# One joined instruction in the float64 conversion, x loaded in 1 KB rows, and a new order of the first loads

## The chip, the cores and the metric

The kernel runs on one core of one Trainium2 chip. The metric is the device time of one execution in microseconds (us). The engines are PE (TensorE matmul; PEld is its weight load), DVE (VectorE), ACT (ScalarE), POOL (GpSimd) and SP (SyncE, which here only issues DMAs).

## The reference, cut to what matters

Attention over 8 batches, 8 heads, 512 rows, 32 state rows and 64 features is followed by two gated products. The weights come as float64 arrays, x and state as float32.

```python
scores = scale * x @ state.T            # [B, H, 512, 32]
xread = softmax(scores, -1) @ state     # each row of x reads the state
sread = softmax(scale * state @ x.T, -1) @ x   # each state row reads x
x = concat([xread, sread], axis=2)      # per batch 544 rows of 512
h = (x @ w1) * (x @ w2) @ w3            # 512 -> 1024 -> 1024
x2 = h @ w_out                          # 1024 -> 512
out = (x2 @ w_a) * (x2 @ w_b) @ w_out2  # 512 -> 1536 -> 512
```

## The kernel before, in words

All tiles of 128 x 1024 four-byte words come from a pool of 47 units; PSUM is a pool of 8 banks. Every large product runs as three passes over a high and a low part (`PASSES`), so that each operand is split by an ACT cast (`high`, L305, or L147) and a subtraction on DVE or POOL (`low`, L311, or L153).

**Start.** The weights w1 and w2 are multiplied by the state before anything else (`state_product`, L326, tile pb), and these products go to DRAM (`p_d`) and come back as chunks pr (`load_p`, L602). w3 and w_out are multiplied into one matrix (`transpose_w3`, L355; `weight_product`, L370, tile wp). Attention of batches 0 and 1 is made beside it, then the first batch's two gated products (`first_product`, tile f, recorded at L1129) and its output (`first_output`, L1366, tile x2f). All of this is a list of `Job` objects, each with an engine, an assumed duration, what it waits for, how many free units and banks it needs and a priority; `run_jobs` puts them in an order by these assumed times, and each engine then executes its instructions in that order. `EARLY` gives the order of the loads on SP: `w3_i` and `woi` are 1 MB pieces of w3 and w_out, `wkp_nh` are halves of the rows of w1 and w2 for two heads, `xb` is batch b. `WO_ORDER`, the order in which a weight product takes its w_out pieces, follows from `EARLY`. `KEEP`, `KEEP_SG`, `LATE_KEEP` and the like say how many units stay free.

**Conversion of float64 (class `Convert`).** A piece of 128 x 512 values has a high word c and a low word d per value. `take` runs two ACT instructions in place (L178 on c, L181 on d), `shift` a DVE instruction (L187, c shifted left by 3 into a new tile) and `add` a POOL instruction (L193, d added). There are 40 such pieces in the start and 52 later, in the intakes sw (w1, w2 once more), ab (w_a, w_b) and z (w_out2), which call `make`.

**Attention.** `load_x_half` brings four heads in four DMAs, with 256-byte runs; `x_transpose` transposes 128 x 128 blocks (two heads of 64 features on the partitions); `scores` multiplies the state's transposed tile `st_s` with it, per head, 64 x 32 weights over 512 columns; `scores_move` copies each of two banks to SBUF on ACT; `maxima`, `col_exp`, `row_shift` and so on are the softmax in both directions. `MIDDLE` and `BEHIND` place these steps of batch b+1 and b+2 between the products of batch b from batch 1 on.

**Later.** `block1` (tiles ap, bp, hfp, hp, x2p) runs batches 1 to 7 and the state rows, 24 passes per step; the intakes and `Features` work beside it. `block2(g)`, four times, holds the second gated product (L1583), its state part for g = 0 (`state_step`, L1666) and the output (L1909). Only g = 0 still has conversions beside it.

Of the kernel before, what the change touches and what calls it, by code (L numbers as in the profile page):

```python
# [9 lines left out]
F32 = mybir.dt.float32  # L10
# [14 lines left out]
    "w3_6 wo0 w3_0 w3_7 wo2 w3_2 w3_4 x0 wo3 w3_3 wo1 "  # L25
    "w3_5 x1 w3_1 wk1_0 wk0_0 wk1_1 x2 wk3_0 wk2_1 wk2_0 wk0_1 wk3_1"
# [38 lines left out]
P_KEEP = 3  # L65
X_SLOT = 0
PASSES = ((0, 0), (0, 1), (1, 0))
# [3 lines left out]
def attention_moe_moe2(  # L71
# [93 lines left out]
    class Convert:  # L165
# [9 lines left out]

        def take(self, i):
            c, d = self.words(i)
            nc.scalar.activation(  # L178
                out=c.bitcast(F32), in_=c.bitcast(F32), func=AF.Prelu, scale=2.0**-112, alpha=2.0**32
            )  # L180
            nc.scalar.activation(out=d.bitcast(I32), in_=d, func=AF.Copy, scale=2.0**-29)  # L181

        def shift(self, i):
            if self.out is None:
                self.out = unit(self.name)[:, : self.n]
            c, out = self.words(i)[0], self.out[:, i * 512 : (i + 1) * 512].bitcast(U32)
            nc.vector.tensor_scalar(  # L187
                out=out, in0=c, scalar1=3, scalar2=None, op0=ALU.logical_shift_left
            )

        def add(self, i):
            d, out = self.words(i)[1], self.out[:, i * 512 : (i + 1) * 512].bitcast(I32)
            nc.gpsimd.tensor_tensor(out=out, in0=out, in1=d.bitcast(I32), op=ALU.add)  # L193
            free(self.raws[i][0])

        def make(self):
            for i in range(len(self.raws)):
                self.shift(i)
                self.add(i)
# [23 lines left out]
    def load_x_half(b, g):  # L223
        t = unit(f"x{b}_{g}")
        v = t.rearrange("p (t h d) -> p t h d", h=4, t=NT)
# [19 lines left out]
    st_s = unit("stT")  # L245

# [31 lines left out]
    def state_move(bg):  # L278
        nc.scalar.copy(st_s[:, bg * 512 : (bg + 1) * 512], st_b[bg])
# [109 lines left out]
    class Attention:  # L389
# [5 lines left out]
        def x_transpose(self, g):  # L395
            self.xt.append(flat(unit(f"xt{self.b}_{g}"), S))
            for j in range(2):
                t = self.banks[g, j] = bank(f"xt{self.b}_{g}_{j}")
                for n in range(NT):
                    nc.tensor.transpose(  # L400
# [1576 lines left out]
```

## Time and profile before

| | us |
|---|---|
| median of 3 runs (1310.37 to 1311.49) | 1310.57 |
| the profiled execution | 1310.82 |
| its span, first to last instruction | 1309.0 |
| PE busy in the span | 1275.8 |
| DVE, ACT, POOL busy | 748.8, 584.4, 582.2 |

PE is busy for 97% of the span, and its granted clock is 0.994 on average. The span therefore has 33 us in which PE does nothing, and the question for each stage is how much of these lie in it and who ends them.

### The profile page before, as it was taken

How to read it: one execution, taken by the hardware profiler on the slowest of the kernel's cores; microseconds unless marked ns; L12 is line 12 of the kernel's file. 1: busy time of each engine (PE TensorE's matmuls, PEld its weight loads, DVE VectorE, ACT ScalarE, POOL GpSimd, SP SyncE). 2: the span in 40 equal slices, each digit the busy share in tenths (PEclk: the TensorE clock that was granted, in tenths of full speed). 3: DMA queues.
4: the chain of work that ended last, by engine and by line, in shares of the span. 5: the costliest groups of instructions: out<-in, count | busy, mean ns of one | idle time of the engine just before them, and what ended most of it. 6: DMA issues, size and time to landing. Idle time of an engine off the chain costs nothing.

```text
span 1309.0 us, 19764 instructions
## 1 busy us (share of the span) xinstructions
PE 1275.8 (97%) x7514; PEld 1079.3 (82%) x7514; DVE 748.8 (57%) x861; ACT 584.4 (45%) x956; POOL 582.2 (44%) x398
## 2 busy tenths in 40 slices
PE   6998999999999999999999999999999999999998
PEld 4765777878877888988879998889988889988898
DVE  5896044767566667555656853247922369433493
ACT  7896355555555666455433431123511235212232
POOL 5674125545355487367348341148411274212450
PEclk7999999999999999999999999999999999999999
DMA  9988695564676642698574779317695247873271
GB/s 305 291 246 260 186 269 181 178 176 137 193 221 206 216 142 86 250 304 275 193 289 145 250 257 386 113 36 248 222 405 175 65 166 260 339 270 107 81 257 66
DMA packets 155134, 276.56 MB, mean 211 GB/s; under 512 B 47136, under 2 KB 92192, under 8 KB 155040
## 3 DMA queue, kind: packets, MB, share of 16 engines
q1 hardware_dynamic: 150752, 260.09, 60.1%
q0 software_dynamic: 4288, 15.21, 3.0%
q8 instruction: 60, 0.98, 0.3%
q14 instruction: 34, 0.28, 0.1%
HBM read 205.00 MB, written 70.25 MB: 210 GB/s over the span
## 4 chain that ended last, share of the span: by engine, by line
PE 81%; DVE 3%; ACT 2%; DMA 2%; issue 1%; POOL 1%; SPq 0%; ACTq 0%
PE r L1583 19%; PE ro L1909 10%; PE x2p L1188 10%; PE v L1583 9%; PE vo L1909 5%; PE bp L1129 5%; PE ap L1129 5%; PE q L1583 5%; PE qo L1909 2%; PE abs L1666 2%; PE x2f L1366 2%; PE srv L1848 1%; PE pb L326 1%; PE bs L1129 1%; DMA zr<-in_moe_w_out_dram 1%
## 5 line engine op out<-in xcount | busy, mean ns | idle before, releaser
L1772 POOL TENSOR_TENSOR r<-e,e 128x512 f32<-128x512 f32 x48 | 63.6, 1325 | 278.5 <-DVE e L1597 278.5
L1188 PE MATMUL x2p<-hp,ws 128*128 128x512 f32 x672 | 161.9, 390 | 0.0
L1188 PEld LDWEIGHTS x2p<-hp,ws 128*128 128x128 f32 x672 | 125.7, 188 | 26.3
L153 POOL TENSOR_TENSOR pl<-pr,ph 128x512 fp32r<-128x512 f32 x64 | 84.5, 1341 | 137.1 <-ACT ph L147 106.2
L1717 ACT COPY e<-r 128x512 f32<-128x512 f32 x48 | 28.2, 588 | 188.7 <-PE r L1583 188.6
L1780 DVE TENSOR_TENSOR r<-e,r 128x512 f32<-128x512 f32 x48 | 33.0, 687 | 128.8 <-PE r L1583 128.8
L1153 DVE TENSOR_TENSOR hfp<-asbp,bp 128x512 f32<-128x512 f32 x56 | 38.2, 683 | 82.7 <-PE bp L1129 81.6
L153 DVE TENSOR_TENSOR hp<-hfp,hp 128x512 fp32r<-128x512 f32 x56 | 55.2, 986 | 41.9 <-ACT hp L147 41.2
L1597 DVE TENSOR_TENSOR e<-e,q 128x512 f32<-128x512 f32 x48 | 32.9, 685 | 73.3 <-PE q L1583 73.3
L1621 POOL TENSOR_TENSOR r<-r,r 128x1024 f32<-128x1024 f32 x24 | 70.9, 2967 | 2.2 <-issue 1.2
L1583 PE MATMUL r<-xT3h,w 128*128 128x512 f32 x192 | 67.1, 390 | 2.0 <-ACT e L1745 2.0
L1583 PE MATMUL r<-xT4h,w 128*128 128x512 f32 x192 | 67.3, 391 | 1.2 <-DVE e L1597 1.2
L1583 PE MATMUL r<-xB11h,w 128*128 128x512 f32 x192 | 67.0, 390 | 0.2 <-DMA w<-w_d 0.2
L1583 PE MATMUL r<-xT2h,w 128*128 128x512 f32 x192 | 67.2, 390 | 0.0
L1583 PE MATMUL q<-xB21h,w 128*128 128x512 f32 x192 | 66.9, 389 | 0.0
L1583 PE MATMUL v<-xB22h,w 128*128 128x512 f32 x192 | 66.9, 389 | 0.0
L1583 PE MATMUL v<-xT1h,w 128*128 128x512 f32 x192 | 66.9, 389 | 0.0
L147 ACT CAST hp<-hfp 128x512 fp32r<-128x512 f32 x56 | 34.7, 619 | 62.5 <-DVE hfp L1153 61.1
L1745 ACT COPY e<-r 128x512 f32<-128x512 f32 x48 | 28.2, 588 | 70.8 <-PE r L1583 70.8
L1147 ACT COPY asbp<-ap 128x512 f32<-128x512 f32 x56 | 33.0, 589 | 49.7 <-PE ap L1129 49.7
L1597 DVE TENSOR_TENSOR e<-e,v 128x512 f32<-128x512 f32 x48 | 32.9, 685 | 29.2 <-PE v L1583 22.8
L1129 PE MATMUL bp<-ah,ph 128*128 128x512 f32 x112 | 47.9, 428 | 0.3 <-DVE a L485 0.3
(503 smaller groups left out, 3821.5 us busy)
## 6 DMA issues: line engine op xcount, KB each, us to landing
w<-w_d SPq DMA_DIRECT2D x132, 512.0 KB, 7.9
zz<-z_d SPq DMA_DIRECT2D x84, 512.0 KB, 4.4
w_d<-w SPq DMA_DIRECT2D x96, 256.0 KB, 3.4
p_d<-sg SPq DMA_DIRECT2D x128, 128.0 KB, 2.6
pr<-p_d SPq DMA_DIRECT2D x32, 512.0 KB, 5.5
w<-w_d SPq DMA_DIRECT2D x36, 256.0 KB, 9.0
x<-in_x_dram SPq DMA_DIRECT2D x64, 128.0 KB, 4.5
sw<-in_moe_w_dram SPq DMA_DIRECT2D x16, 512.0 KB, 5.1
```

The lines of the kernel that those rows point to most:

```text
L147: nc.scalar.copy(hi, src)
L153: (eng or nc.vector).tensor_tensor(out=lo[:, i], in0=src[:, i], in1=hi[:, i].bitcast(F32), op=ALU.subtract)
L1129: nc.tensor.matmul(dst[:, :n], lhsT=l[m], rhs=r[q], start=i == 0 and j == 0, stop=i == k - 1 and j == 2,)
L1147: nc.scalar.copy(a_sb[:, :n], pa[:, :n])
L1153: nc.vector.tensor_tensor(out=hf[:, :n], in0=a_sb[:, :n], in1=pb[:, :n], op=ALU.mult)
L1188: nc.tensor.matmul(acc[j], lhsT=w_s[f][:, m, j * P : (j + 1) * P], rhs=h[:, q, :n], start=per == 1 and f == 0 and i == 0, stop=f == NF1 - ...
L1583: nc.tensor.matmul(t, lhsT=w[m], rhs=xf[g].parts[x][q][:, k, :], start=first and k == 0 and i == 0, stop=k == 1 and i == 2, skip_group_che ...
L1597: nc.vector.tensor_tensor(out=out, in0=x, in1=y, op=ALU.add)
L1621: ENGINES[eng].tensor_tensor(out=out, in0=x, in1=y, op=op)
L1772: nc.gpsimd.tensor_tensor(out=h[1], in0=e2, in1=e5, op=ALU.mult)
L1780: nc.vector.tensor_tensor(out=h[0], in0=e1, in1=r, op=ALU.mult)
L1909: nc.tensor.matmul(dst, lhsT=hl[m][:, k, i * P : (i + 1) * P], rhs=z[:, k, q, :], start=FIRST[p] and j == 0 and k == 0 and i % 2 == 0 and ...
```

## The change

1. The conversion's last two steps become one DVE instruction (`join`: shift c left by 3, then OR with d), for all 92 pieces; POOL's add goes. So that an OR does, d's scale is reduced (`LAST_BITS`).
2. In the start, d's step (`last_bits`) may run on ACT or POOL, the casts `high` and the copies of x (`x_part`) on ACT or DVE, whichever the plan finds earlier. In the intakes `take` stays on ACT.
3. x comes with one DMA for four heads, in runs of 1 KB. After the transposes the partitions then hold two neighbouring rows of one head. Each head's scores are made from both halves of the partitions, so there is a second state tile with the halves exchanged (`stX`, two DVE copies from PSUM for each of two groups), `scores` issues 16 products of 256 columns in place of 8 of 512, and `scores_move` writes in pieces of 128 columns.
4. The order of the loads, the priorities and the units kept free are new. The state is loaded behind the first w3 piece, not between its halves. The third load is a w_out piece, x of batch 0 the fourth, an attention weight the sixth; the last two are `wk0_0` and `w3_0`.
5. A transposed half of w3 waits for its own half's conversion only. The intake z looks 2.0 us ahead in place of 1.5.

```diff
 EARLY = (
-    "w3_6 wo0 w3_0 w3_7 wo2 w3_2 w3_4 x0 wo3 w3_3 wo1 "
-    "w3_5 x1 w3_1 wk1_0 wk0_0 wk1_1 x2 wk3_0 wk2_1 wk2_0 wk0_1 wk3_1"
+    "w3_6 w3_3 wo3 x0 w3_4 wk0_1 wo0 x2 w3_7 x1 wo1 "
+    "wo2 wk1_1 wk2_0 w3_2 w3_5 wk1_0 wk3_1 wk3_0 wk2_1 w3_1 wk0_0 w3_0"
 ).split()
...
-WP_PRIO = 1
-PRIO = 0.06
-KEEP = 9
-KEEP_SG = 2
-KEEP_UNTIL = 40
-STORE_FIRST = 6
+WP_PRIO = 6
+STATE_AT = 1
+PRIO = 0.03
+KEEP = 10
+KEEP_SG = 1
+KEEP_UNTIL = 30
+STORE_FIRST = 18
...
-LATE_KEEP = 6
-LATE_PRIO = 10
+LATE_KEEP = 4
+LATE_PRIO = 4
...
+        def top(self, i):
+            c = self.words(i)[0].bitcast(F32)
+            nc.scalar.activation(out=c, in_=c, func=AF.Prelu, scale=2.0**-112, alpha=2.0**32)
+
+        def last_bits(self, i, eng="A"):
+            d = self.words(i)[1]
+            if eng == "A":
+                nc.scalar.activation(out=d.bitcast(I32), in_=d, func=AF.Copy, scale=LAST_BITS)
+            else:
+                nc.gpsimd.tensor_scalar(
+                    out=d.bitcast(I32), in0=d, scalar1=LAST_BITS, scalar2=None, op0=ALU.mult
+                )
+
...
-            nc.vector.tensor_scalar(
-                out=out, in0=c, scalar1=3, scalar2=None, op0=ALU.logical_shift_left
+            c, d = self.words(i)
+            nc.vector.scalar_tensor_tensor(
+                out=self.out[:, i * 512 : (i + 1) * 512].bitcast(U32),
+                in0=c,
+                scalar=3,
+                in1=d,
+                op0=ALU.logical_shift_left,
+                op1=ALU.bitwise_or,
             )
-
-        def add(self, i):
-            d, out = self.words(i)[1], self.out[:, i * 512 : (i + 1) * 512].bitcast(I32)
-            nc.gpsimd.tensor_tensor(out=out, in0=out, in1=d.bitcast(I32), op=ALU.add)
             free(self.raws[i][0])
...
-        for h in range(4):
-            nc.sync.dma_start(
-                out=v[:, :, h, :], in_=x[b, 4 * g + h].rearrange("(p t) d -> p t d", t=NT)
-            )
-        x_n[b, g] = t.rearrange("p (t c e) -> p t c e", t=NT, c=2)
+        v = t.rearrange("p (h n) -> p h n", h=4)
+        nc.sync.dma_start(
+            out=v, in_=x[b, 4 * g : 4 * g + 4].rearrange("h (p t) d -> p h (t d)", t=NT)
+        )
+        x_n[b, g] = t.rearrange("p (c r n) -> p c r n", c=2, r=2)
...
+    def state_swap(bg):
+        part = slice(bg * 512, (bg + 1) * 512)
+        for r in range(2):
+            nc.vector.tensor_copy(st_x[(1 - r) * D : (2 - r) * D, part], st_b[bg][r * D : (r + 1) * D])
...
-            for p in range(NP):
-                for r in range(2):
-                    rows = slice(r * D, (r + 1) * D)
-                    nc.tensor.matmul(
-                        self.banks[r][NS * p : NS * (p + 1), :],
-                        lhsT=st_s[rows, c + p * P : c + p * P + NS],
-                        rhs=self.xt[p // 2][rows, p % 2, :],
-                        start=True,
-                        stop=True,
-                    )
+            for r in range(2):
+                for p in range(NP):
+                    for w in range(2):
+                        rows = slice(w * D, (w + 1) * D)
+                        nc.tensor.matmul(
+                            self.banks[w][NS * p : NS * (p + 1), r * 256 : (r + 1) * 256],
+                            lhsT=(st_s, st_x)[r ^ w][rows, c + p * P : c + p * P + NS],
+                            rhs=self.xt[p // 2][rows, p % 2, r * 256 : (r + 1) * 256],
+                            start=True,
+                            stop=True,
+                        )
...
-            t = Job("A", 1.3, lambda i=i: conv[name].take(i), after=[l], prio=2)
-            s = Job("V", 0.75, lambda i=i: conv[name].shift(i), after=[t] + adds, need=1 - i, prio=2)
-            adds = adds + [Job("G", 1.3, lambda i=i: conv[name].add(i), after=[s], prio=2)]
+            t = Job("A", 0.7, lambda i=i: conv[name].top(i), after=[l], prio=2)
+            d = Job("AG", (0.7, 1.75), lambda e, i=i: conv[name].last_bits(i, e), after=[l], prio=2)
+            adds = adds + [
+                Job("V", 0.72, lambda i=i: conv[name].join(i), after=[t, d] + adds, need=1 - i, prio=2)
+            ]
...
-                    after=list(adds),
+                    after=[adds[k]],
...
-                iz.run(HORIZON[0])
+                iz.run(HORIZON[2])
```

## Rows read from the trace of the kernel before

**Rows 1.** Busy time of each engine by stage, with granted clock, DMA share and GB/s.

```profile
core 0: us, PE busy (x) PEld busy (x) DVE busy (x) ACT busy (x) POOL busy (x), PEclk, DMA share, GB/s
0.00:21.40 21.40, 9.08 (x34) 4.73 (x35) 8.37 (x14) 14.61 (x25) 9.78 (x13) 0.80 0.92 307
21.40:36.30 14.90, 14.44 (x70) 12.02 (x69) 12.79 (x16) 11.21 (x21) 10.23 (x8) 0.83 1.04 309
36.30:98.70 62.40, 62.07 (x331) 42.87 (x330) 55.15 (x73) 57.05 (x108) 42.61 (x30) 1.00 0.87 264
98.70:134.00 35.30, 29.80 (x193) 20.83 (x187) 21.71 (x23) 22.49 (x42) 13.11 (x10) 1.00 0.85 261
134.00:167.10 33.10, 33.10 (x145) 22.22 (x145) 1.98 (x3) 13.93 (x28) 3.80 (x4) 1.00 0.61 185
167.10:546.10 379.00, 374.60 (x2304) 305.65 (x2303) 235.70 (x297) 220.52 (x386) 197.78 (x156) 1.00 0.60 186
546.10:784.50 238.40, 232.62 (x1454) 209.31 (x1453) 149.30 (x187) 101.27 (x157) 127.94 (x86) 1.00 0.71 244
784.50:1309.00 524.50, 520.08 (x3006) 461.65 (x3004) 263.79 (x251) 143.33 (x195) 177.00 (x92) 1.00 0.56 200
```

**Rows 2.** Waits of PE, 0 to 170 us: for whom, total, times, longest.

```profile
PE w3t L355 <- POOL w L193: 9.8, 3, 5.1
PE f L1129 <- POOL pl L153: 2.2, 5, 1.2
```

**Rows 3.** Timeline of PE: the first weight product and the first gated product.

```profile
21.43 0.78 PE L370 MATMUL wp<-woh,w3h 128*128 128x512 f32 x1
...
108.07 0.50 PE L1129 MATMUL f<-ah,ph 128*128 128x512 f32 x1 [1.18 <-ACT sg L338]
```

**Rows 4.** Timeline of ACT, DVE and POOL: the first w_out piece.

```profile
11.61 0.67 ACT L178 ACTIVATE wo0r<-wo0r 128x512 f32<-128x512 f32 x1 [0.26 <-DMA wo0r<-in_moe_w_out_dram]
...
15.22 0.42 DVE L187 TENSOR_SCALAR wo<-wo0r 128x512 uint32<-128x512 uint32 x1
...
15.77 1.35 POOL L193 TENSOR_TENSOR wo<-wo,wo0r 128x512 int32<-128x512 int32 x1 [1.35 <-ACT w_0r L181]
...
16.08 0.62 ACT L305 CAST woh<-wo 128x512 fp32r<-128x512 f32 x1
...
19.47 1.69 DVE L311 TENSOR_TENSOR wol<-wo,woh 128x512 fp32r<-128x512 f32 x1
```

**Rows 5.** Transfers that landed between 10 and 25 us, then 24 and 36 us.

```profile
DMA packets 2112, 6.09 MB, mean 406 GB/s; under 512 B 655, under 2 KB 655, under 8 KB 2112
...
DMA packets 4865, 3.39 MB, mean 283 GB/s; under 512 B 4293, under 2 KB 4293, under 8 KB 4865
```

**Rows 6.** Timeline of SP: the issue of x of batch 0.

```profile
16.90 10.89 SPq L227 DMA_DIRECT2D x<-in_x_dram  x8
```

**Rows 7.** Busy time of each engine in two stretches of the start.

```profile
15.00:30.00 15.00, 10.42 (x38) 8.30 (x38) 14.75 (x18) 14.71 (x28) 11.36 (x8) 0.62 1.05 339
40.00:90.00 50.00, 49.67 (x254) 36.22 (x254) 46.79 (x59) 46.23 (x88) 38.00 (x27) 1.00 0.84 261
```

**Rows 8.** The same for DVE's shift (L187) alone.

```profile
40.00:90.00 50.00, 20.40 (x23) 1.00 0.84 261
```

**Rows 9.** Groups of DVE instructions, 0 to 135 us: busy, mean ns, idle before.

```profile
L311 DVE TENSOR_TENSOR w3l<-w3t,w3h 128x512 fp32r<-128x512 f32 x16 | 10.8, 681 | 5.2 <-ACT w3h L305 5.2
...
L311 DVE TENSOR_TENSOR wol<-wo,woh 128x512 fp32r<-128x512 f32 x6 | 8.5, 1410 | 0.4 <-ACT woh L305 0.4
```

**Rows 10.** Chain that ended last, 160 to 179 us: start, us, what.

```profile
160.06 7.07 PE pb L326 x32
...
171.47 1.02 PE st L416 x16
...
174.07 2.74 PE x2p L1188 x12
...
178.18 0.58 PE sr L507 x32
```

**Rows 11.** Waits of PE from 170 us to the end: the longest.

```profile
PE r L1583 <- ACT e L1745: 2.0, 2, 1.7
```

More of the change, by code (lines that the diff above doesn't have):

```diff
@@ L197, in make @@
             for i in range(len(self.raws)):
-                self.shift(i)
-                self.add(i)
+                self.join(i)
     def flat(t, c):
@@ L245, in attention_moe_moe2 @@
     st_s = unit("stT")
+    st_x = unit("stX")
     def load_early(n):
@@ L278, in state_move @@
     def state_move(bg):
-        nc.scalar.copy(st_s[:, bg * 512 : (bg + 1) * 512], st_b[bg])
+        part = slice(bg * 512, (bg + 1) * 512)
+        nc.scalar.copy(st_s[:, part], st_b[bg])
+    def state_swap(bg):
+        part = slice(bg * 512, (bg + 1) * 512)
+        for r in range(2):
+            nc.vector.tensor_copy(st_x[(1 - r) * D : (2 - r) * D, part], st_b[bg][r * D : (r + 1) * D])
     flip = [0]
@@ L716, in split_jobs @@
             h = Job(
-                "A",
-                0.6,
-                lambda part=part: high(kind, i, part, conv[name].out[:, part]),
+                "AV",
+                (0.65, 0.72),
+                lambda e, part=part: high(kind, i, part, conv[name].out[:, part], e),
                 after=[adds[k]] + lows,
@@ L806, in attention_jobs @@
             done.append(
-                Job("A", 0.6, lambda g=g: a.scores_move(g), after=[t] + done[2:], need=1 - g, prio=prio).gives("ps", 1)
+                Job("A", 0.6, lambda g=g: a.scores_move(g), after=[t] + done[4:], need=1 - g, prio=prio).gives("ps", 1)
             )
-        mx = Job("V", 2.9, a.maxima, after=done[2:], need=1, prio=prio)
+        mx = Job("V", 2.9, a.maxima, after=done[4:], need=1, prio=prio)
         ce = Job("A", 1.3, a.col_exp, after=[mx], need=1, prio=prio)
@@ L830, in attention_moe_moe2 @@
     wo_done = {}
+    wk_early = {}
     products = []
     w_done = []
-    for name in EARLY:
+    for n_early, name in enumerate(EARLY):
+        if n_early == STATE_AT:
+            state_jobs()
         if name[:2] == "wk":
             p, nh = int(name[2]), int(name[4])
-            early_wk(p, nh)
+            wk_early[p, nh] = early_wk(p, nh)
         elif name[:2] == "wo":
@@ L901, in attention_moe_moe2 @@
             for g in range(2):
-                l = load_job(3.5, lambda b=b, g=g: load_x_half(b, g), 1, 2.0)
+                l = load_job(1.6, lambda b=b, g=g: load_x_half(b, g), 1, 2.0)
                 t = Job("P", 1.8, lambda b=b, g=g: attn[b].x_transpose(g), after=[l], need=1, prio=1, banks=("ps", 2))
-                done.append(
-                    Job("V", 0.9, lambda b=b, g=g: attn[b].x_move(g), after=[t], prio=1).gives("ps", 2)
-                )
+                for j in range(2):
+                    done.append(
+                        Job(
+                            "AV", (0.65, 0.75), lambda e, b=b, g=g, j=j: attn[b].x_part(g, j, e), after=[t], prio=1
+                        ).gives("ps", 1)
+                    )
             if b < 2:
@@ L1514, in behind @@
                 if b == B - 2 and f == NF1 - 1:
-                    free("stT")
+                    free("stT", "stX")
                     split(sr_s[0], sr_s[1], sr, nc.gpsimd)
@@ L1526, in behind @@
                 ab.run(HORIZON[0])
-                iz.run(HORIZON[0])
+                iz.run(HORIZON[2])
             return middle, behind
```

61 lines of the change are left out of this document (32 added, 29 removed).

## Prediction

> **What bounds the kernel now.** I read the busy times by stage first [rows 1]. From 36.3 us on PE is hardly ever idle: 0.3 us up to 98.7, nothing from 134 to 167.1, 4.4 us from there to 546.1, 5.8 us to 784.5 and 4.4 us in the rest. So an engine that is relieved there gives nothing by itself; only PE's own instructions and the few stalls count. The losses lie at the front. Up to 21.4 us PE has almost nothing to do, since its first weight product starts at 21.43 us [rows 3]. From 21.4 to 36.3 us it is idle for 0.5 us, but the granted clock is 0.83 on average between its levels of 1.2 and 2.4 GHz, so that a further 14.9 x 0.17 = 2.5 us go. From 98.7 to 134 us it is idle for 35.30 - 29.80 = 5.5 us.
>
> The waits say who is late there. In the first stage PE's transposes of w3 wait 9.8 us for POOL's add, the last link of the conversion [rows 2]. The timeline of the first w_out piece shows the same chain [rows 4]: its first half lands at 11.6 us, the second half's shift runs at 15.22 and its add at 15.77, the first half's cast at 16.08 behind other pieces' `take`, and the last subtraction at 19.47, drawn out to 1.69 us. ACT and DVE are full from 15 to 30 us, 14.71 and 14.75 of 15 us [rows 7]. From 98.7 on PE waits for chunks of p_d: for POOL's low part (2.2 us), and the first gated product starts only at 108.07 us, behind ACT's copies [rows 2, 3].
>
> **The change part by part.** The sum is made against the profiled execution; its 1310.82 us are 0.25 above the median, which is less than I can resolve, so the gains are taken from the median, 1310.57.
>
> *Conversion.* Per piece the shift (0.42 us where POOL is quiet) and the add (1.35 us) go [rows 4]. The join is not in the trace. It reads two SBUF operands. The nearest rows are DVE's subtraction with one operand in PSUM, 0.681 us, and that with both in SBUF, 1.41 us while POOL works [rows 9]. I take 0.7: what drew out the 1.41 and the 1.69 was POOL at work, and POOL loses its 92 adds. The link of two engines, 0.42 + 1.35 = 1.77 us and a handover, thus becomes 0.7 us. On DVE the shifts of 40 to 90 us took 20.40 us for 23 [rows 8], 0.887 each, since most met POOL; joins at 0.7 need 16.1 us, at 1.41 they need 32.4 us. The Trainium skill speaks against this step: "GPSIMD Engine Reference", in its table of specifications, says that POOL shares its SBUF interfaces with VectorE instructions that have two SBUF inputs, as the join has. The two subtraction rows agree. By that rule alone, POOL as busy as before, the joins cost the upper figure; that is the third rival.
>
> *`last_bits` on POOL* has no row; the nearest, POOL's 1.35 us add, also walks 512 words, and 0.67 us on ACT is the lower bound. I take 1.35. It is parallel to ACT's own step, so it is hidden as long as ACT has other pieces to do, which the 14.71 of 15 us say [rows 7]; without that cover it costs the piece 1.35 - 0.67 = 0.7 us.
>
> *The first w_out piece.* It is loaded behind w3_6, the state and w3_3, 1.05 MB later in the queue than now. At 406 GB/s [rows 5] that is 2.6 us; the 8% of the first 21.4 us in which DMA is not busy [rows 1] are at most 1.7 us, which the earlier second half of w3_6 can use. Its first half lands at 12.5 to 14.2 us, the second 0.52 MB or 1.3 us later. Then come one step of `take` 0.67, join 0.7, cast 0.62, subtraction 0.7: 2.7 us, or 3.3 if both steps of `take` stay on ACT. That is 16.5 to 18.8 us without queueing. Of the present 9.8 us from landing to product some 4 are queueing; I leave 1.5 of them and say 19.2 us: 2.2 us gained. Ends: 0 and 4.9 us.
>
> *21.4 to 36.3 us.* 3.0 us are lost here. x of batch 0 arrives in it: the transfers run at 283 GB/s, against 406 before them, with 4293 of 4865 packets under 512 B [rows 5], and its issue holds SP for 10.89 us [rows 6]. With 1 KB runs I expect a rate nearer to 406; the megabyte then takes 2.6 us in place of some 4 or 5, and SP issues two DMAs, not eight. ACT gives up casts and last bits to DVE and POOL. Against it, only one of four w_out pieces is there until the seventh load, so PE lives on one product of 6 passes (6 x 0.228 = 1.4 us, by the pitch of [rows 10]) for each of three w3 pieces, on transposes, scores and the state products of the early attention weight. I take 2.0 of the 3.0 us. Ends: 0 and 3.0.
>
> *98.7 to 134 us.* The last loads are now wk0_0 and w3_0, so that when the last store of the chunks' first half is under way, PE still has w3_0's 24 passes (24 x 0.228 = 5.5 us) and the second state products, of which 32 passes or 7.07 us stand unused until 160 us now [rows 10]. With LATE_KEEP lower they may come sooner. That is 12.5 us of cover for 5.5 us of idle time. I take 3.5; ends 0 and 5.5. PE's own work from 134 on is unchanged.
>
> *After 167 us.* The 4.4 us behind 784.5 are left as they are: no conversion is left there. Of the 10.2 us between 167 and 784.5, some come from conversions that queue ahead of what PE needs (the longest wait is for an ACT copy, 2.0 us in 2 times [rows 11]). A chain shorter by 1.1 us for each half, and DVE no longer drawn out, are worth 1.5 us, by an estimate; ends 0 and 5.
>
> *Scores.* 16 records of 512 columns take 1.02 us now, 64 ns each; 32 of 256 columns follow. By columns that stays 1.02 us, by records it becomes 2.04. The reads, 32 records of 64 columns in 0.58 us, 18 ns each [rows 10], show that records as such are not the limit at 64 ns. I take 0.1 us more for each of 8 batches, since all of it is PE's own: 0.8 us lost; ends 0 and 8.2. Here too the Trainium skill has a rule that speaks against the change: "TensorE: Matmul & The Clock Gate", section "Wait — 56ns, not 53.3ns?", gives about 62 ns of issue per matmul with hardware decode off. By that figure 32 records need 1.98 us, 7.7 us more over 8 batches; the reads at 18 ns contradict it for this program.
>
> *The rest at nothing.* The two state_swap pairs are four DVE copies of 0.68 us each at most, 2.7 us, before the first scores; they lie in a stretch where PE waits for weights, and without that cover cost 2.7 us once. The strided `scores_move` and the 1 KB transposes have the same counts and sizes. stX takes one unit of 47, which delays a load if units run short.
>
> Sum: 2.2 + 2.0 + 3.5 + 1.5 - 0.8 = 8.4 us, so 1310.57 - 8.4 = 1302.2 us.
>
> **The rivals.**
>
> *More is recovered.* All upper ends hold: 4.9 + 3.0 + 5.5 + 5 = 18.4, less 0.8: 1293 us. For it: every idle stretch has one named cause that the change touches. Against it: the plan's order follows assumed times, and some handovers remain. Chance 0.13.
>
> *The gain is given back.* PE is full from 36 to 98.7 us. If the first gated product still hangs on the chunks of the last attention weight, which now lands later (the last load but one, where an attention weight of the other half stood last), the earlier start only makes the wait before it longer: 2.2 + 2.0 + 3.5 vanish, 1.5 - 0.8 remain: 1309.9 us. For it: the 108.07 us start already hangs on that chain. Against it: the 12.5 us of cover. Chance 0.07.
>
> *DVE becomes the bound (slower).* Place: 40 to 90 us, where DVE is busy 46.79 of 50 us [rows 7]. Price: joins at 1.41 us need 12.0 us more than the shifts; 3.2 are free, so PE is 8.8 us late, and with DVE as the limit the 4.2 us of the early start go too. 1310.6 + 8.8 - 3.5 - 1.5 + 0.8 = 1315.2 us. It decides from a join of 0.887 + 3.2 / 23 = 1.03 us on. For it: subtractions with two SBUF operands took up to 1.69 us beside POOL, and casts and copies are moved onto DVE. Against it: POOL, 38.00 of 50 us busy there [rows 7], loses 23 adds of 1.35 us, 31 us. Chance 0.14.
>
> *Scores cost by record:* 8.2 us in place of 0.8, which takes back 7.4: 1309.6 us. Chance 0.05.
>
> **How the numbers follow.** The forecast, 4 to 14 us faster, has 0.61: 1302.2 us, by itself 1297 to 1306.5. A measurement of this kernel can tell about 0.2%, 2.6 us. Faster by more: 0.61 + 0.13, and a hundredth of the others, 0.75. Same: 0.07 + 0.05 less that, 0.11. Slower: 0.14. The range reaches up to the two cases without change and down to all upper ends: 1293 to 1310; outside stay the slower case and the tip of the larger gain.
>
> **What would show it.** Right: the first wp record near 19 us; joins of 0.7 us, POOL under 25 us busy between 40 and 90; less than 2 us of idle PE between its last wp and x2f; st in 1.0 to 1.1 us with 32 records; x transfers with about 1 MB in 3 us. Wrong: a wp start no earlier than 21 us, joins over 1.03 us with DVE full, gated products that wait longer than now for pr, or st near 2 us. The prediction as a whole fails if PE starves again between 30 and 98 us, which it does not now.

## The result and the profile after

The changed kernel takes 1323.97 us (median of 4 runs, 1322.62 to 1325.25) against 1310.8 for the kernel before beside it: 1.0102 times the time, 95% interval 1.0087 to 1.0117. It is 13 us slower, where 8.4 us faster was forecast. The profiled execution has a span of 1322.4 us, 13.4 more than before.

The busy times by stage answer to [rows 1]. They are cut where stages begin in this kernel: the first weight product at 19.9 us, the first gated product f at 119.4, the first gated product of batch 1 (ap) at 175.8, the first product of the second block at 563.3. What lies before ap is called the start from here on, and the stretch from ap to the second block the first block:

```profile
core 0: us, PE busy (x) PEld busy (x) DVE busy (x) ACT busy (x) POOL busy (x), PEclk, DMA share, GB/s
0.00:19.90 19.90, 12.67 (x51) 8.87 (x51) 11.88 (x20) 13.12 (x22) 2.79 (x8) 0.68 0.94 300
19.90:36.30 16.40, 14.17 (x104) 9.38 (x102) 12.58 (x16) 13.12 (x27) 12.60 (x8) 0.97 1.05 384
36.30:90.00 53.70, 46.41 (x280) 31.07 (x280) 43.51 (x62) 38.18 (x71) 34.86 (x22) 0.94 0.86 290
90.00:119.40 29.40, 29.40 (x122) 15.75 (x121) 10.99 (x15) 19.11 (x36) 5.04 (x4) 1.00 0.82 236
119.40:144.90 25.50, 25.50 (x109) 18.50 (x107) 9.39 (x14) 14.66 (x25) 7.62 (x6) 1.00 0.64 197
144.90:175.80 30.90, 30.90 (x131) 20.41 (x129) 2.78 (x3) 11.17 (x21) 4.38 (x4) 1.00 0.54 159
175.80:563.30 387.50, 377.75 (x2399) 308.40 (x2398) 232.12 (x305) 222.56 (x392) 151.78 (x120) 1.00 0.57 184
563.30:800.20 236.90, 234.25 (x1467) 211.89 (x1466) 143.53 (x180) 96.67 (x150) 105.95 (x70) 1.00 0.69 238
800.20:1322.40 522.20, 517.43 (x2995) 459.44 (x2993) 263.02 (x250) 142.75 (x194) 177.01 (x92) 1.00 0.55 199
```

Set against [rows 1] (first block from 167.1 to 546.1), the 13.4 us come about thus. The first block starts at 175.8 us, 8.7 later. It takes 387.5 us, 8.5 more. From its end to the first state product (srv, at 724.7 us, 711.9 before) 161.4 us pass in place of 165.9: 4.5 us come back. What follows takes 0.6 us more.

The start is the instructive part. PE waits no longer than before: the busy times up to the first block add up to 159.05 of 175.8 us, 16.8 idle, against 148.49 of 167.1, 18.6 idle. So 10.6 us went into PE's own instructions, though their work is nearly the same. Idle time has moved too: 7.3 us of it now lie between 36.3 and 90 us, where there had been next to none. At 85 us PE had made 126 of the 192 weight products; before, all 192 were done. The waits of PE between 36.3 and 90 us, and two short stretches of it with busy times and granted clock:

```profile
PE xt L419 <- ACT a L512: 2.6, 1, 2.6
PE pb L344 <- ACT s L453: 2.4, 1, 2.4
PE w3t L373 <- DVE w L199: 1.6, 1, 1.6
PE wp L388 <- DVE w3l L329: 1.1, 1, 1.1
...
38.10:41.50 3.40, 3.11 (x39) 2.42 (x40) 3.37 (x5) 2.85 (x7) 2.33 (x2) 0.50 1.02 406
85.90:89.30 3.40, 3.40 (x11) 2.30 (x11) 3.40 (x5) 1.03 (x4) 0.00 (x0) 0.50 0.52 153
```

The first wait ends at 38.4 us, the second at 84.2, and in the two stretches the granted clock is 0.50, the lower of its two levels. In the start of the kernel before it is at that level from 12.9 to 26.5 us only; in the changed kernel from 7.4 to 21.0 us and in these two stretches. PE is busy for 16.0 us at the lower level, 7.9 before.

The timeline of PE shows what the instructions look like now. In the changed kernel:

```profile
19.86 0.78 PE L388 MATMUL wp<-woh,w3h 128*128 128x512 f32 x1
...
94.04 1.13 PE L344 MATMUL pb<-wk,stT 64*128 64x512 f32 x4
95.10 0.50 PE L388 MATMUL wp<-woh,w3h 128*128 128x512 f32 x1
95.43 0.40 PE L388 MATMUL wp<-wol,w3h 128*128 128x512 f32 x1
...
96.69 1.13 PE L344 MATMUL pb<-wk,stT 64*128 64x512 f32 x4
```

and in the kernel before:

```profile
83.35 12.29 PE L326 MATMUL pb<-wk,stT 64*128 64x512 f32 x56
```

Before, most state products (pb, matmuls of 64 rows) stood in runs, 0.22 us each. Now they stand in fours among weight products (128 rows). Four take 1.06 us by the starts, not 0.88, and the six weight products between them 1.59 us, not the 1.37 of six at 0.228.

Several steps went as forecast. The first weight product starts at 19.86 us. DVE's joins in 40 to 90 us, the row that answers to [rows 8]:

```profile
40.00:90.00 50.00, 20.93 (x28) 0.95 0.84 281
```

are 0.75 us each, and DVE is 40.22 of these 50 us busy, before 46.79 [rows 7]. The x rows came out as said: the issue of x of batch 0 holds SP for 1.46 us in place of 10.89 [rows 6], that of the other two batches for 1.88 and 1.95, and DMA moves 381 GB/s between 24 and 36 us, with 140 packets under 512 B, against 283 with 4293 [rows 5]. The 32 score records of a batch take 1.0 us.

### The profile page after: what moved, and what is told of

Its sections match the earlier page's. It is cut to its first block, busy times and chain, and to the rows that moved or that the text cites. A ratio compares the mean times of both kernels' runs of the same rounds, so it can differ in the third digit from the quotient of the medians.

```text
span 1322.4 us, 19820 instructions
## 1 busy us (share of the span) xinstructions
PE 1288.5 (97%) x7642; PEld 1083.7 (82%) x7642; DVE 729.8 (55%) x862; ACT 571.3 (43%) x933; POOL 502.0 (38%) x332
## 5 line engine op out<-in xcount | busy, mean ns | idle before, releaser
L155 DVE TENSOR_TENSOR hp<-hfp,hp 128x512 fp32r<-128x512 f32 x56 | 46.5, 830 | 42.4 <-ACT hp L149 42.4
```

Source lines behind the costliest of these rows:

```text
L155: (eng or nc.vector).tensor_tensor(out=lo[:, i], in0=src[:, i], in1=hi[:, i].bitcast(F32), op=ALU.subtract)
```

## The experiments

**Theory for the start:** the new priorities and reserves scatter the state products, and each change between matmuls of 64 and of 128 rows costs PE time. Rivals: the new order of loads starves PE; or the last-bits step on POOL is late. **Theory for the first block:** joins, and the sums behind them, queue on DVE ahead of what PE waits for. Rivals: the planner's changed charge (the time of POOL that it assumes for a conversion, `G=2.4` before, none after), the x rows and strided copies, the wider look-ahead for wo2 (the intake z).

Behind each time stands its ratio to the kernel before, run beside it, and the 95% interval of that ratio. "Start" with a time says when the first block begins. Stretches are read from one profiled execution of each kernel.

### The start

**e_old_order**: the changed kernel with the old EARLY list, priorities and reserves.

```diff
-EARLY = ("w3_6 w3_3 wo3 x0 ..."); WP_PRIO = 6; PRIO = 0.03; KEEP = 10; ... LATE_KEEP = 4; LATE_PRIO = 4
+EARLY = ("w3_6 wo0 w3_0 w3_7 ..."); WP_PRIO = 1; PRIO = 0.06; KEEP = 9; ... LATE_KEEP = 6; LATE_PRIO = 10
```

> The changed kernel with the load order, priorities and unit reserves of before (the state still behind the first piece). If the new order starves PE in the start (theory order), the first gated product of batch 1 (first ap) comes at 160 to 167 us, in place of 175.8, and the time falls by 8 to 12 us to 1312 to 1316; the rest of the loss, about 5 us or more between first ap and the second block, stays. If the conversion dealt to POOL is what starves PE (theory POOL bits), first ap stays at 172 us or later and the time at 1320 or more.

Measured: 1314.36 us (1.0025, interval 1.0015 to 1.0034). The first block starts at 166.9 us, 8.9 earlier than in the changed kernel. The plan, not the new instructions, cost the start. But those instructions bring nothing there: the first weight product is at 18.1 us, 3.3 earlier than before, the last one 2.5 earlier, the first gated product of batch 0 2.0, its last 1.0, the first of batch 1 0.2. The head start melts at each link, among others in 2.1 us of waits for ACT's sn and 1.5 for its ph.

**e_order_alone**: the kernel before with the new order, priorities and reserves alone.

> The kernel before with the new order of loads, priorities and reserves alone (and the late state products made to wait for the early ones, without which this plan can't be laid out); conversion and x as before. Theory order: the order is bad by itself, so first ap comes at 175 to 185 us, in place of 167.1, the state products of the start stand in over 20 groups between the weight products (8 before), and the stretch to the second block stays at 379 us: 1319 to 1330. Rival: the order is only bad with the dealt steps; first ap at 165 to 169 us, 1309 to 1313.

Measured: 1330.94 us (1.0152, 1.0137 to 1.0167); first block at 188.2 us, then 378.3 us for it, no loss there. The plan alone costs 21 us in the start; the rest of the change wins 12 of them back.

**e_old_early** (old list of loads, new priorities) and **e_new_early** (new list, old priorities) cut the plan in two.

> The changed kernel with the old order of loads, but the new priorities and reserves. If the order of loads starves PE: first ap at 165 to 170 us and 1313 to 1317, though state products may still be scattered. If the priorities do it (state products ahead of weight products, in many small groups, each of which costs PE some 0.4 us): over 20 groups, PE's instructions of the start take 155 us or more without its idle time (150.7 with all old, 159.3 with all new), first ap at 171 to 176 us, 1318 to 1324.

Measured: 1322.17 us (1.0084, 1.0069 to 1.0099), start 175.1 us, 21 groups: as the second reading has it.

> The changed kernel with the new order of loads, but the priorities and reserves of before. The start with old order and new priorities was 175.1 us, with both old 166.9. If the priorities alone cost the 9 us, the first block starts at 166 to 169 us and the time is about 1314 to 1316. Rival: the order of loads costs as much by itself, since only one of four w_out pieces is there until the seventh load; then the start is 172 us or later and the time above 1319.

Measured: 1321.41 us (1.0074, 1.0060 to 1.0087), start 171.7 us, the first gated product at 119.3. Neither extreme held. The priorities alone cost 8.2 us against e_old_order, the list alone 4.8, both together 8.9.

**e_late**: the changed kernel, two numbers as before.

```diff
-LATE_KEEP = 4
-LATE_PRIO = 4
+LATE_KEEP = 6
+LATE_PRIO = 10
```

> The changed kernel with the reserve and the priority of the second state products alone as before (LATE_KEEP 6, LATE_PRIO 10). If it is these two numbers that scatter the second state products among the weight products, their groups fall from 26 to about 8 to 12, PE's own time before the first block from 159 to about 151 us, and the first block starts 6 to 8 us earlier, near 168 us; the time falls by as much, to about 1316. Rival: the scattering comes from WP_PRIO and PRIO (the weight products give way to everything else); then the start stays within 2 us of 175.8 and the time near 1323.

Measured: 1321.29 us (1.0072, 1.0059 to 1.0086), start 170.9 us, 18 groups of state products in place of 26, not the 8 to 12 expected: over half of the start's loss is gone with these two numbers, not all of it.

**e_act_bits**: the changed kernel with last_bits on ACT only in the start.

```diff
-d = Job("AG", (0.7, 1.75), lambda e, i=i: conv[name].last_bits(i, e), after=[l], prio=2)
+d = Job("A", 0.7, lambda i=i: conv[name].last_bits(i), after=[l], prio=2)
```

> The changed kernel with the last bits of every piece of the start on ACT. Theory POOL bits: these take 1.55 to 2.06 us on POOL against 0.67 on ACT and stand there behind other work, so first ap comes 4 to 8 us earlier and the time is 1316 to 1320. Theory order: ACT only gets fuller, first ap between 174 and 180 us, the time 1322 to 1328.

Measured: 1331.84 us (1.0161, 1.0145 to 1.0178), start 181.7 us, with one PE wait of 7.3 us for DVE's w3l; both readings had it lower. Dealing the last bits to POOL helps the start by 6 us in this plan, although a step there is dear. The groups of POOL in the changed kernel, 40 to 90 us:

```profile
L187 POOL TENSOR_SCALAR wk_1r<-wk_1r 128x512 int32<-128x512 uint32 x6 | 9.8, 1637 | 1.3 <-DMA wk_1r<-in_moe_w_dram 1.0
L187 POOL TENSOR_SCALAR wk_0r<-wk_0r 128x512 int32<-128x512 uint32 x4 | 6.5, 1634 | 2.3 <-DMA wk_0r<-in_moe_w_dram 2.0
```

**e_switch** prices the change of rows by itself: the kernel before with matmuls added ahead of the last pair's first product; their results are not read.

```diff
+wide(24)       # 128 rows x 512 columns
+narrow(24)     # 64 rows x 512 columns, upper and lower half in turn
+for i in range(6):
+    wide(6)
+    narrow(4)
```

> The kernel before with 84 further matmuls whose results nobody reads, ahead of the first product of the last pair: 24 of 128 rows in a run, 24 of 64 rows (upper and lower rows in turn) in a run, then six times 6 of 128 rows and 4 of 64 rows. If going from one kind to the other has a price of its own, the two runs take about 0.22 us for each matmul and the alternation 12 or 13 times 0.1 to 0.25 us more than 60 x 0.22 = 13.2 us, that is 14.5 to 16 us. Rival: the price in the changed kernel came from waits or the clock there; then the alternation takes 13.2 to 13.6 us.

Its timeline of PE:

```profile
781.04 5.63 PE L1742 MATMUL tw<-xB11h 128*128 128x512 f32 x24
786.61 3.04 PE L1747 MATMUL tp<-xB11h 64*128 64x512 f32 x24
789.57 1.66 PE L1742 MATMUL tw<-xB11h 128*128 128x512 f32 x6
791.16 0.73 PE L1747 MATMUL tp<-xB11h 64*128 64x512 f32 x4
791.83 1.67 PE L1742 MATMUL tw<-xB11h 128*128 128x512 f32 x6
...
802.42 0.73 PE L1747 MATMUL tp<-xB11h 64*128 64x512 f32 x4
803.09 0.50 PE L1583 MATMUL r<-xB11h,w 128*128 128x512 f32 x1
```

From start to start, a wide one in the run takes 5.57 / 24 = 0.232 us, a narrow one 2.96 / 24 = 0.123. By that six rounds would be 6 x (6 x 0.232 + 4 x 0.123) = 11.3 us; they take 803.09 - 789.57 = 13.52. The total alone lies where I had put the rival, since I had taken 0.22 us for a narrow one; against the runs beside it, 2.2 us are paid for 12 changes, 0.19 us each, with no wait between. That is a lower bound, since each of the two runs ends in a change as well. Inside the runs a wide one starts 0.227 us after the last, and the narrow ones start in pairs, upper and lower half together, every 0.229 us; by that the rounds would take 10.9 us, and a change costs 0.22. The first record behind a change starts 0.32 us after the last one, and the next one of the new kind another 0.33 us later. The Trainium skill states a rule that fits, in "TensorEngine Tiling (Array Packing)", section "Key Properties": a change of the tiling mode drains TensorE. It gives no price; this trace does.

Counted from the PE records ahead of ap, with PE's busy and idle time up to there:

```
kernel        changes 64/128 rows  groups of pb  PE busy, us  idle, us  first block at, us
before                 15                7          148.5       18.6        167.1
e_old_order            17                8          150.4       16.5        166.9
e_new_early            26               12          153.3       18.4        171.7
e_late                 39               18          154.7       16.2        170.9
e_old_early            45               21          158.3       16.8        175.1
after                  55               26          159.1       16.8        175.8
e_act_bits             50               23          160.5       21.2        181.7
e_order_alone          49               23          165.9       22.3        188.2
```

40 more changes at 0.19 to 0.22 us are 7.4 to 8.7 us, of the 10.6 us that PE's busy time grew by. The records bear this out: from start to start and without the waits, weight and state products together take 84.1 us in place of 76.5, 7.6 more. The rest goes with the clock: the 8.1 us more that PE is busy at half of the clock are worth some 4 us, by an estimate that takes its work there as twice as long, and the transposes of x alone take 7.9 us in place of 4.9. The two terms overlap, and no run isolates the clock. But e_old_order has the mean clock of the changed kernel in the start, 0.94, with 38 changes and 8.7 us of busy time less. The last two kernels of the table also wait more, and e_order_alone's busy time is higher than its changes explain.

### The first block

The stretch meant here runs from the first gated product of batch 1, ap (two of the expectations call it the first score), to the first product of the second block: 378.9 us before, 387.5 after. PE's idle time grows from 4.4 to 9.8 us in it, and the waits for DVE do it. The two largest in the changed kernel, then the largest for DVE in the kernel before:

```profile
PE xt L419 <- DVE xt L430: 4.2, 4, 1.5
PE bs L1164 <- DVE hfp L1188: 2.8, 3, 1.5
...
PE bs L1129 <- DVE hfp L1153: 0.7, 1, 0.7
```

**e_join**: the kernel before with the join alone, shift and add gone, and POOL no longer charged for an intake's conversion.

```diff
-self.shift(i); self.add(i)
+self.join(i)
-(1, dict(V=1.2, G=2.4), lambda: o["c"].make()),
+(1, dict(V=1.2), lambda: o["c"].make()),
```

> The kernel before with the joined instruction alone: shift and OR on DVE in all 92 pieces, no add on POOL, both other steps on ACT; order, x and parameters as before. If the join is a gain by itself, first ap comes at 160 to 166 us and the time is 1303 to 1310. Theory plan: the stretch from first ap to the second block is 4 to 9 us longer than the 379 us of before, which takes the start's gain back: 1309 to 1318. If DVE becomes the bound, first ap later than 167 us and the time above 1314.

Measured: 1329.84 us (1.0142, 1.0123 to 1.0160). Start 167.5 us, the stretch 384.9, and from there to the first state product 181.5 us in place of 165.9, with one PE wait of 18.1 us. The join with its lighter charge costs 6 us in the first block, and something worse in the second, to which I come back.

The timeline of the changed kernel, batch 3, shows how. POOL's `al`, DVE and PE:

```profile
312.19 1.25 DVE L199 SCALAR_TENSOR_TENSOR ab<-ab 128x512 uint32<-128x512 uint32 x2
...
313.03 0.39 PE L1164 MATMUL bp<-ah,pl 128*128 128x512 f32 x1
...
313.43 2.73 POOL L155 TENSOR_TENSOR al<-a,ah 128x512 fp32r<-128x512 f32 x2 [6.79 <-ACT ah L149]
313.47 2.97 DVE L1013 TENSOR_TENSOR ab9s<-ab 128x256 f32<-128x256 f32 x2
...
317.15 0.68 DVE L1188 TENSOR_TENSOR hfp<-asbp,bp 128x512 f32<-128x512 f32 x1
...
319.13 0.68 DVE L430 COPY xt<-xt 128x512 f32<-128x512 f32 x1
...
319.96 0.63 PE L419 MATMUL xt<-ident,x 128*128 128x128 f32 x4 [1.41 <-DVE xt L430]
```

The join is done at once, so the sums of `ab` follow it directly and meet POOL's two `al` halves. Two sums of 0.42 us take 2.97. PE's bp is there at 313.4 us, but hfp, queued behind the sums, runs at 317.15; the copy of xt comes later still, and PE waits. Before, the sums waited for POOL's own add, which was over at 314.90 us, stood behind hfp and the copy of xt, and ran beside an idle POOL:

```profile
L978 DVE TENSOR_TENSOR ab9s<-ab x2: 417/418/418, 316.2 to 316.6; 128x256 f32<-128x256 f32 x2
```

The Trainium skill, "SBUF — State Buffer", section "SBUF: two separate sides", describes an exclusive lock: a DVE instruction with two SBUF inputs and a GpSimd one that reads SBUF block one another for their whole length. The rows agree: 2.97 us for two sums beside 2.73 for two halves of `al`.

**e_plan_g**: the changed kernel with `dict(V=1.2, G=2.4)` for the intakes again.

> The changed kernel; only the planned time of the later conversions counts 2.4 us of POOL again, as before, so that the order of the later stages is planned as before though POOL's add is gone. Theory plan (DVE gets the intakes' instructions ahead of what PE waits for, since the plan thinks them ready sooner): the stretch from first ap to the second block's first product falls from 387.5 towards 379 us, the time to 1315 to 1319; the start is unchanged at 175.8. Rival: the loss there comes from the start's leftovers or the x layout, and the stretch stays at 385 to 389 us, the time at 1322 to 1325.

Measured: 1325.50 us (1.0111, 1.0084 to 1.0139), the stretch 390.1. The stretch does not fall, so the charge by itself is not the cause. (The profiled execution took 1329.68 us, 4.2 more than the median, so 390.1 is a high value.) With it, 16 of wo2's sums stand in the first block in place of 12, at 0.62 us each in place of 0.42.

**e_sums_pool**: the changed kernel with all sums of `ab` on POOL (`e = nc.gpsimd`, charged 2.6 us).

> The changed kernel with the sums of the w_a and w_b intake always on POOL (every second piece's stood on DVE). Theory DVE pile: the join makes these sums ready at once, so joins and sums stand in one row of up to 6 us on DVE ahead of hfp and of the copy of the transposed x, and PE waits at the last step of batches 3 and 4. Without the sums the stretch from first ap to the second block falls from 387.5 to 379 to 383 us and the wait of xt for DVE from 4.2 to under 1.5 us: 1316 to 1320. Rival: the joins alone are too long for DVE there; the stretch stays above 385 us, 1322 to 1326.

Measured: 1322.96 us (1.0091, 1.0074 to 1.0108), the stretch 383.4: about half of the loss gone, in batches 3 and 4; batch 7 loses as before. Little of it shows in the time, against the 1316 to 1320 expected: the stretch behind the first block takes 163.3 us in place of 161.4.

**e_best**: e_old_order with the same sums on POOL.

> The changed kernel with the old order and parameters and these sums on POOL. If the order and the DVE pile are the two causes, both are gone: first ap at 166 to 168 us, a stretch of 379 to 383 us, and the gain of 3 to 4 us between the second block's first product and the state part stays: 1304 to 1310, at or below the kernel before. If the pile is not the cause, 1313 to 1316.

Measured: 1313.38 us (1.0020, 1.0011 to 1.0029), the stretch 382.7. Still slower than before.

**e_hybrid**: e_old_order, with shift and add again for the intakes of w1, w2, wa and wb; wo2 stays joined, and its look-ahead stays at `HORIZON[2]`.

> The changed kernel with the order and priorities of before, and with the intakes of the first block and the second (w1, w2, wa, wb) converted by shift on DVE and add on POOL as before, planned with POOL's time; joins stay in the start and for wo2's second use. If the loss in the first block comes from joins and sums that meet on DVE, the stretch from the first score to the first product of the second block falls from 385.5 to 378 to 380 us; with the start at 167 and the rest as in the changed kernel that is 1307 to 1309 us, faster than both. Rival: the loss comes from elsewhere (the new plan of the look-ahead, the x rows); the stretch stays at 383 us or more and the time at 1313 to 1315.

Measured: 1321.64 us (1.0074, 1.0058 to 1.0091), the stretch 393.6, the longest of all. A clear miss, and it points to wo2's work as the other part. One of its lines, with POOL's split beside it:

```profile
325.08 3.69 DVE L1125 TENSOR_TENSOR zs<-z 128x256 f32<-128x256 f32 x1
...
325.94 2.54 POOL L155 TENSOR_TENSOR w<-ab,w 128x512 fp32r<-128x512 f32 x2
```

A difference of 128x256 elements that takes 0.41 us by itself takes 3.69 here.

**e_b1_add**: the changed kernel; every conversion begun before the second block is shift and add as before, with the old charge and the old look-ahead for wo2.

```diff
+late = in_block2[0]
-(1, dict(V=1.2), lambda: o["c"].make()),
+(1, dict(V=1.2) if late else dict(V=1.2, G=2.4), lambda: o["c"].make(late)),   # make: join if late, else shift and add
-iz.run(HORIZON[2])
+iz.run(HORIZON[0])
```

> The changed kernel, start and order unchanged, with every conversion that is begun before the second block done as before (shift on DVE, add on POOL, planned with POOL's time, wo2's look-ahead as before); later ones stay joined. If the loss in the first block comes from joins and sums with two SBUF operands that DVE runs while POOL works, the stretch from the first score to the first product of the second block falls from 387.5 to 378 to 381 us, DVE's sums there from up to 1.5 us to 0.42 us each, and the time to about 1316; the stretch behind it stays near 162 us. Rival: the loss comes from the x rows, the strided copies or the units of the new layout; the stretch stays at 384 us or more, the time at 1320 or more.

Measured: the stretch is 378.5 us: the whole loss is gone, with x rows, strided copies and the new layout still in place. So they are free, and the conversion with its charge and the look-ahead are the cause, together. Two of the sums of `ab` still take 1.50 us each here, so a drawn-out sum costs only where something that PE needs stands behind it. The time, 1333.40 us (1.0177, 1.0160 to 1.0194), is worse all the same: the next stretch takes 180.4 us, again with a wait for wo2.

**e_b2_join**: the same with the start of e_old_order.

> The same with the order and the priorities of before in the start. By the same theory: start 166 to 167 us, stretch 378 to 381 us, from there to the first state product 162 to 163 us, and the rest as before, 598.7 us: 1305 to 1309 us, faster than before. Rival: block 1 keeps the loss for another reason; 1312 us or more.

Measured: 1325.57 us (1.0110, 1.0095 to 1.0125): start 166.6, the stretch 378.9, the next 182.8 us.

**e_b2_z**: e_b2_join with the wider look-ahead for wo2 in the first block.

```diff
-iz.run(HORIZON[0])
+iz.run(HORIZON[2])
```

> As e_b2_join, but with the wider look-ahead for wo2 in the first block that the changed kernel has. If that look-ahead is what keeps wo2's last pieces from coming late in the changed kernel, the 18.9 us wait falls below 2 us and the stretch behind the first block to 161 to 163 us; the first block then carries more of wo2's sums and takes 379 to 385 us: 1306 to 1312 us. Rival: the look-ahead does not matter; the wait stays over 10 us.

Measured: 1318.68 us (1.0067, 1.0053 to 1.0081). The late wait is gone (0.7 us, the stretch behind the first block 161.1 us), and the first block takes 391.9 us: this one edit costs 12.9 us there. DVE's sums of wo2 in that block:

```profile
L1128 DVE TENSOR_TENSOR zs<-z 128x256 f32<-128x256 f32 x8 | 7.5, 943 | 0.0
L1128 DVE TENSOR_TENSOR zs<-z,zs 128x256 f32<-128x256 f32 x8 | 6.6, 822 | 0.1
```

16 at 0.88 us, in place of 8 at 0.41 to 0.42 in the kernel before. The second block gets 4.8 of the 12.9 us back.

Four of these kernels, all with the old order of loads, make a table of the two edits in the first block: 378.9 us with neither (e_b2_join), 384.9 with the join and its lighter charge (e_join, x in its old rows), 391.9 with the look-ahead (e_b2_z), 385.5 with both (e_old_order). Beside joins the look-ahead thus adds 0.6 us, not 12.9. The trace of the changed kernel agrees: it has 12 of wo2's sums in the first block, and none is drawn out, 0.41 to 0.42 us each. So in the change as made most of the loss goes with the join; up to 387.5 us the rest comes with the new plan of the start, by a path that no run isolates.

### The second block

**e_last_join**: the kernel before with joins for conversions begun in the second block only, and the lighter charge there.

> The kernel before with joins only for the conversions that are begun in the second block; start, x rows, scores and first block unchanged. If the changed kernel's gain of 4.5 us behind the first product of the second block comes from the join alone (no wait for POOL's add), that stretch falls from 165.9 to 161 to 163 us and the time to 1306 to 1308 us. Rival: the gain there is only what the late first block had left to do earlier; the stretch stays at 165 to 166 us and the time within 0.1% of 1310.6.

Measured: 1326.21 us (1.0117, 1.0102 to 1.0132), the stretch behind the first block 181.1 us. The wait, as e_b2_join shows it, and the last loads of wo2's words (SP's timeline) in e_b2_join:

```profile
PE ro L1960 <- DMA zz<-z_d: 18.9, 1, 18.9
...
676.61 7.16 SPq L164 DMA_DIRECT2D zr<-in_moe_w_out_dram  x2
```

and in the kernel before:

```profile
656.07 0.87 SPq L162 DMA_DIRECT2D zr<-in_moe_w_out_dram  x2
```

**e_b2_plan** and **e_last_plan**: e_b2_join and e_last_join with the planner still charging POOL for the later conversions, though they are joined.

```diff
-(1, dict(V=1.2) if late else dict(V=1.2, G=2.4), lambda: o["c"].make(late)),
+(1, dict(V=1.2, G=2.4), lambda: o["c"].make(late)),
```

> As e_b2_join (order and priorities of before, conversions of the first block by shift and add, later ones joined), but the planner goes on charging POOL 2.4 us for each later conversion, so that intakes start as in the kernel before. In e_b2_join the first block was as before (378.9 us) and 18.9 us went in one wait for the last piece of wo2, whose load was issued at 683 us in place of 656. If the plan alone made it late, the wait is gone: stretch 378.9, then 162 to 164 us since no conversion waits for POOL's add: 1306 to 1309 us, faster than before by 0.1 to 0.35%. Rival: the joins themselves let wa and wb run ahead and hold the units that wo2 needs; then the wait stays over 10 us and the time at 1320 or more.

Measured: 1308.08 us (0.9984, 0.9975 to 0.9992).

> The kernel before with joins only for conversions begun in the second block, and its plan untouched (POOL still charged). By the same theory the 18.4 us wait is gone and the waits for POOL there (3 to 4 us) too: 1306.5 to 1309 us. Rival: as above, 1320 or more; or the join brings nothing there, 1310 to 1311.

Measured: 1309.02 us (0.9989, 0.9981 to 0.9998). In both the last loads of wo2 come as early as before (655.11 us in e_b2_plan) and the wait is 1.3 and 1.1 us. So the lighter charge let other intakes go first, and wo2 came late. These two are the only kernels here that are faster than the kernel before, by 2.1 and 1.2 us between the medians; that is less than the 0.2% that I named as the bound, but neither interval reaches 1. The stretch behind the first block takes 164.3 and 163.5 us in place of 165.9: joins alone are worth 1.6 to 2.4 of the 4.5 us that the changed kernel gains there, and the rest goes, as far as e_b2_z's 161.1 us tell, with wo2's work done earlier. The stages of e_b2_plan:

```profile
0.00:166.20 166.20, 150.91 (x788) 105.07 (x788) 100.34 (x135) 106.79 (x195) 60.88 (x46) 0.94 0.75 254
166.20:545.00 378.80, 374.44 (x2399) 307.54 (x2398) 232.54 (x296) 220.38 (x386) 198.06 (x156) 1.00 0.58 188
545.00:783.40 238.40, 234.08 (x1462) 210.66 (x1461) 151.13 (x187) 101.63 (x159) 105.86 (x70) 1.00 0.71 246
783.40:1306.50 523.10, 518.66 (x3000) 460.60 (x2998) 263.65 (x251) 142.68 (x194) 176.85 (x92) 1.00 0.56 200
```

## Why the prediction was wrong

**First weight product** (2.2 us gained): right, 1.6 in the changed kernel, 3.3 with the old order. The join at 0.7 us was right too, 0.68 where POOL is quiet and 0.75 on average from 40 to 90 us. The rival by which DVE becomes the bound there did not come about: 40.22 of 50 us busy.

***last_bits* on POOL**: mis-sized. I took 1.35 us from POOL's add; it takes 1.54 to 2.09, and POOL is 31.9 us busy from 40 to 90, not under 25. It did not decide: DVE waits for it for 4.0 us in the whole start, and with all of it on ACT the start is 5.9 us later (e_act_bits).

**21.4 to 36.3 us and 98.7 to 134 us** (2.0 + 3.5 us gained): this is the step that failed in the start. I counted the state products and w3_0's passes as "12.5 us of cover", at the price that they have in a run, and looked only at how long PE would be idle. They did fill the gap: from 90 to 175.8 us PE is never idle. But they filled it in fours, at 0.19 to 0.22 us for each change of rows, and 7.3 us of idle time came up before 90 us, which I had named as the sign of failure, with the lower clock beside it. That idle time comes with the new list as with the new priorities (4.8 us in e_new_early, 5.8 in e_old_early, 0.5 in e_old_order); who set it off is not isolated. The rival with the right place, the gain given back at 1309.9 us, had no price for PE's own time. The one with the right sign, DVE as the bound at 1315.2 us, would have been right by luck: its mechanism is not there. Without the new plan the start gains 0.2 us, not 7.7: the links between the first weight product and batch 1 took the head start.

**After 167 us** (1.5 us gained): this is the second step that failed. The sign was wrong, 4.6 us are lost: 8.5 in the first block and 0.6 at the end, less 4.5 in the second. I gave the shorter chain as a gain wherever it stands, and put the two-operand contention that I had read in [rows 9] in the start alone. In the first block it puts joins and sums on DVE while POOL works: 6 us by the join with its charge (e_join). And one edit had no term at all: wo2's look-ahead, from `HORIZON[0]` to `HORIZON[2]`. e_b2_z shows it to cost 12.9 us in the first block with shift and add, but 0.6 beside joins: the two do not add. The lighter charge, which I did not price either, would have cost another 18 us in the second block had that look-ahead not been there; with it, 4.5 us are gained.

**Scores** (0.8 us lost): right in kind, 32 records in 1.0 us; no loss is to be seen. In the first block e_b2_plan has 2399 PE records and is 374.4 us busy, the kernel before 2304 and 374.6 [rows 1]. The x rows' transfers were right and worth nothing in time: e_b2_plan, with them and all the rest of the new conversion, starts its first block 0.6 us earlier than e_last_plan without.

What is only read from timelines, not isolated: that each lost microsecond of the first block is a collision of the kind shown in batch 3. Undoing conversion, charge and look-ahead removes the loss; which of the colliding pairs carries how much stays open, and of the 8.6 us only 5.4 are idle time of PE, while its busy time grows by 3.3. It also stays open why the list of loads alone costs 4.8 us with 9 more changes of rows; 1.9 of the 4.8 us are idle time.

## What to carry to other kernels

Work that fills a wait has a price of its own: look at where it is put between other instructions, not only at how much there is. An engine's time in a stage is to be forecast as busy plus idle, and a change of plan can raise the one while it lowers the other.

A faster link moves what follows it to another time; ask beside which engine's work it will then run, and what stands in the queue behind it. And a planner's charge is a schedule, not a description: keep it when the operation gets cheaper, until the new order has been looked at for itself.

## What the runs showed of the hardware that was not expected

Changing between matmuls of 64 and of 128 rows cost 0.19 to 0.22 us each way on average, without a wait in the records (e_switch). In a run, 64-row fp32r matmuls of 512 columns, upper and lower half in turn, started in pairs every 0.229 us; 128-row ones started every 0.227. The state products, whose operands are float32, took 0.42 us for a pair.

POOL's multiplication of 128x512 words from uint32 to int32 at every second word took 1.54 to 2.09 us in the changed kernel, ACT's same step 0.64 to 0.71.

A DVE sum or difference of 128x256 with both operands in SBUF took 0.41 to 0.42 us alone, 1.5 us beside one of POOL's splits and 3.69 us at worst (e_hybrid).
